# A layer with linear memory: twelve score tiles of a head group in four blocks of three, TensorE's order fixed, masks first

## Chip, cores and metric

The kernel runs on one core of one Trainium2 chip. The metric is device time in microseconds of one execution, as the median of several runs. A core has five engines with queues of their own: TensorE (PE: matmuls; PEld: its weight loads), VectorE (DVE), ScalarE (ACT), GpSimd (POOL) and SyncE (SP), which here issues most DMAs. TensorE writes only to PSUM; VectorE and ScalarE read PSUM and write SBUF.

## The reference

Four layers in the order A, B, A, B on a residual stream x of 2048 tokens by 640. An A layer is attention within four segments of 512 tokens, 32 heads of 20, mixed with a linear memory that is carried from segment to segment:

```python
for s in range(N):                       # 4 segments of L = 512
    logits = jnp.einsum('bhqd,bhkd->bhqk', qs, ks) * scale + mask
    p = _softmax(logits, axis=-1)
    a_dot = jnp.einsum('bhqk,bhkd->bhqd', p, vs)
    pq = phi(qs)                         # phi(t) = t + 1 where t > 0, else exp(t)
    num = jnp.einsum('bhld,bhde->bhle', pq, M)
    den = jnp.einsum('bhld,bhd->bhl', pq, z)[..., None] + 1e-06
    o = g * (num / den) + (1.0 - g) * a_dot
    pk = phi(ks)
    M = M + jnp.einsum('bhld,bhle->bhde', pk, vs)
    z = z + jnp.einsum('bhld->bhd', pk)
...
x = x + _A_ref(_layernorm(x, axis=-1), A_wq, A_wk, A_wv, A_wo, A_beta)
x = x + _B_ref(_layernorm(x, axis=-1), B_mem0, B_Wq, B_Wk, B_Wv, B_Wo, B_seg_len)
```

The mask is causal within the segment. B layers, which the change doesn't touch, are a recurrence over 64 short segments.

## The kernel before

`layer_A` takes the four segments one after the other. In each, the 32 heads are worked in eight groups of four, so that a layer is a loop over 32 groups `g` (`n` is the segment, `G` the group in it), plus two rounds to finish. The loop is a software pipeline (lines 456 to 505): iteration `g` projects q and k of group g+1, computes score tiles of group g, the probabilities of groups g-2 and g-1, and the product with v of group g-2.

Heads lie 32 rows apart, so a group fills 128 rows, and a pair of heads uses two strips of 32 rows of TensorE's array at a time (`tile_position`). A group has two pairs, and a pair p has these tiles, each of two PSUM banks, from a pool of three (`psx`, tag x):

- three S tiles (`s_round`, line 355; matmuls line 372): scores with the queries along the partitions. They serve only for the row maxima, which VectorE takes with reductions (line 375). The causal mask is put in first, by a matmul of the identity with a table of large negative numbers (line 366), and the scores are added to it. Tile 0 holds the last 128 queries against 512 keys, tile 1 two parts (384 and 128 keys), tile 2 one of 256.
- three T tiles (`t_round`, line 394; matmuls line 407): scores with the keys along the partitions, from a copy of q to which the negated maximum has been added (`q_with_max`, line 382). ScalarE takes the exponential into SBUF (line 410), and GpSimd zeroes what is above the diagonal (line 412).

A group so has six S tiles and six T tiles. S of pair p and T of pair p-3 come together; the two pairs lie on different rows of the array. An iteration has six rounds (two halves with `r` = 0, 1, 2), each with one S and one T tile: masks, S matmuls, T matmuls, and then some of the other products:

- `proj_q` (QP, line 276; ScalarE copies to qT and, from segment 1 on, takes EQ, from which VectorE makes phiq), `proj_k` (KP, line 295; ScalarE copies to kT), `proj_v` (VP, line 306; ScalarE copies to one of three `vaug`)
- `q_with_max` (Q2, lines 386 and 388; ScalarE copies to q2)
- `phi_k` (KN, line 318: transposes of k; ScalarE EK, GpSimd clamps it, VectorE phik; all but the last segment)
- `state` (line 327): the read from the memory (NUM, line 333, from segment 1 on; ScalarE copies to nsb, VectorE and GpSimd divide), and the memory's update (UP, line 348, all but the last segment; VectorE masks it, GpSimd adds it)
- `pv` (PV, line 424, 40 matmuls; ScalarE copies to osb), `norm` (VectorE and GpSimd)
- for the segment before, in groups 2 to 5: `out_stage_a` (otps, line 248, transposes; ScalarE copies to oT) and `out_stage_b` (YP, line 259, two halves of 320 columns; VectorE adds x, line 261; two stores on SP's queue)
- for the segment after, in groups 0, 1 and 6: `seg_load` (a load on SP's queue and a layer norm on VectorE and GpSimd, lines 80 to 87) and `seg_tr` (tps, line 236, transposes; ScalarE copies them to xnT)

All these products share a second PSUM pool of two places (`pg`, tag pg, one bank each): a new one must wait until the tile that held its place has been read.

No order is written out for layer A: `A_ORDERED` is False, so a planner arranges each engine's instructions when the program is built, by their order in the source and by its own idea of when each is ready. On the chip each engine then runs its list in that order. In layer B all engines follow the source (`_OrdNC`).

Of the kernel before, what the change touches and what calls it, by code (L numbers as in the profile page):

```python
# [28 lines left out]
D = 640  # L29
# [131 lines left out]
def layer_A(nc, tc, C, W, x_src, x_dst, src_is_bf16, nseg=4, out_bf16=False, xb_dst=None, load_w=None, side_loads=None):  # L161
    SC = 1.0 / math.sqrt(20.0)
    nc_raw = nc
    if A_ORDERED:
        nc = _OrdNC(tc, nc_raw, engines=ORDER_ENGINES)
    NGR = 8 * nseg
    KOFF = (0, 640, 1024, 512)
    assert not out_bf16
    with ExitStack() as ctx:
# [48 lines left out]
        SEG = {}  # L218

        def seg_load(n_, tt):  # L220
            d = SEG.setdefault(n_, {"xn": [None] * 4, "oT": [None] * 4, "xr": [None] * 4})
            r0 = n_ * 512 + tt * 128
            xt = pxt.tile([128, 2 * D] if src_is_bf16 else [128, D], BF16 if src_is_bf16 else F32, name="a_xt")
            nc.sync.dma_start(xt[:, 0:D], x_src[r0:r0 + 128, :])
            xn = pxn.tile([128, D], BF16, name="a_xn")
            layernorm_tile(nc, sml, C, xt[:, 0:D], xn[:], "a_ln")
            d["xn"][tt] = xn
# [20 lines left out]
                nc.tensor.transpose(tps[:, c, :], d["Onat"][:, tt, 128 * c:128 * c + 128], C.identb[:])  # L248
            nc.scalar.copy(oT[:], tps[:])

        def out_stage_b(n_, tt):
            d = SEG[n_]
            oT, xr = d["oT"][tt], d["xr"][tt]
            r0 = n_ * 512 + tt * 128
            xnew = w1l.tile([128, D], F32, name="a_xnew") if src_is_bf16 else xr
            for half in range(2):
                YP = pg.tile([128, 320], F32, name="a_YP", tag="pg")
                for c in range(NCH):
                    nc.tensor.matmul(YP[:], lhsT=oT[:, c, :], rhs=W.wo[:, c, 320 * half:320 * half + 320],
                                     start=(c == 0), stop=(c == NCH - 1))  # L260
                nc.vector.tensor_tensor(out=xnew[:, 320 * half:320 * half + 320], in0=YP[:], in1=xr[:, 320 * half:320 * half + 320], op=ALU.add)
            nc.sync.dma_start(x_dst[r0:r0 + 128, :], xnew[:])
# [61 lines left out]
            nc.vector.scalar_tensor_tensor(out=pk[:, :, :, 0:20], in0=KNv, scalar=0.0, in1=EK[:], op0=ALU.max, op1=ALU.add)  # L324
            GS[g]["pk"] = pk

        def state(g):
            n, G = divmod(g, 8)
            s_ = GS[g]
            if n >= 1:  # L330
                NUM = pg.tile([128, 4, 4, 32], F32, name="a_NUM", tag="pg")
                for tt in range(4):
                    nc.tensor.matmul(NUM[:, tt, :, :].rearrange("p j s -> p (j s)"), lhsT=s_["phiq"][:, 128 * tt:128 * tt + 128],
                                     rhs=MZb[:, G, :], start=True, stop=True)
                nsb = w1.tile([128, 4, 4, 21], F32, name="a_nsb")
                nc.scalar.copy(nsb[:], NUM[:, :, :, 0:21])
# [6 lines left out]
                s_["am"] = am  # L343
            if n <= nseg - 2:
                UP = pg.tile([128, 128], F32, name="a_UP", tag="pg")
                pk, va = s_["pk"], s_["va"]
                for tt in range(4):
                    nc.tensor.matmul(UP[:], lhsT=pk[:, tt, :, :].rearrange("p j s -> p (j s)"),
                                     rhs=va[:, tt, :, :].rearrange("p j s -> p (j s)"), start=(tt == 0), stop=(tt == 3))
# [5 lines left out]
        def s_round(p, r):  # L355
            g, pr = divmod(p, 2)
            s_ = GS[g]
            if pr == 0 and r == 0:
                s_["nm"] = sm.tile([128, 4, 4], F32, name="a_nm", tag="nm")
            qT, kT, nm = s_["qT"], s_["kT"], s_["nm"]  # L360
            X = psx.tile([128, 2, 512], F32, name="a_S", tag="x")
            m0, m1, parts = ((384, 512, ((3, 0, 512),)),
                             (256, 512, ((2, 0, 384), (0, 384, 128))),
                             (128, 256, ((1, 0, 256),)))[r]
            for e in range(2):
                nc.tensor.matmul(X[:, e, m0:m1], lhsT=C.identb[:], rhs=C.negu[:, 0:(m1 - m0) // 128, :].rearrange("p a k -> p (a k)"),
                                 start=True, stop=False, skip_group_check=True)
            for qc, o, w_ in parts:
                for e in range(2):
                    j = 2 * pr + e  # L370
                    rows = slice(32 * j, 32 * j + 32)
                    nc.tensor.matmul(X[:, e, o:o + w_], lhsT=qT[rows, 128 * qc:128 * qc + 128], rhs=kT[rows, 0:w_],
                                     start=False, stop=True, tile_position=(32 * j, 0), skip_group_check=True)
            for qc, o, w_ in parts:
                nc.vector.tensor_reduce(out=nm[:, qc, 2 * pr:2 * pr + 2], in_=X[:, :, o:o + w_], axis=AX.X, op=ALU.max, negate=True)  # L375

        def negmax_rows(g):
# [13 lines left out]
            nc.scalar.copy(q2[:], Q2[:])  # L391
            s_["q2"] = q2

        def t_round(p, r):
# [5 lines left out]
            Y = psx.tile([128, 2, 512], F32, name="a_T", tag="x")  # L400
            parts = (((0, 0, 512),), ((3, 0, 128), (1, 128, 384)), ((2, 0, 256),))[r]
            width, diag = ((512, 1), (512, 2), (256, 1))[r]
            for n_, (kc, o, w_) in enumerate(parts):
                for e in range(2):
                    j = 2 * pr + e
                    rows = slice(32 * j, 32 * j + 32)
                    nc.tensor.matmul(Y[:, e, o:o + w_], lhsT=kT[rows, 128 * kc:128 * kc + 128], rhs=q2[rows, 128 * kc:512],  # L407
                                     start=True, stop=True, tile_position=(32 * j, 0), skip_group_check=True)
            b = 512 * r
            nc.scalar.activation(out=PT[:, :, b:b + width], in_=Y[:, :, 0:width], func=ACT.Exp, scale=SC)  # L410
            dv = PT[:, :, b:b + 128 * diag].rearrange("p e (a q) -> p e a q", q=128)
# [36 lines left out]
        for tt in range(4):  # L448
            seg_load(0, tt)
            if tt == 1:  # L450
                load_w()
            seg_tr(0, tt)
        proj_q(0)
        proj_k(0)

        for g in range(NGR + 2):
            n, G = divmod(g, 8)
            for half in range(2):
                p = 2 * g + half
                for r in range(3):  # L460
                    if g < NGR:
                        s_round(p, r)
                    if 0 <= p - 3 < 2 * NGR:
                        t_round(p - 3, r)
                    k = (half, r)
                    if k == (0, 0) and g + 1 < NGR:
                        proj_q(g + 1)
                    if k == (0, 1):
                        if 0 <= g - 1 < NGR:
                            q_with_max(g - 1)  # L470
                        if n >= 1 and 2 <= G <= 5 and n <= nseg:
                            out_stage_a(n - 1, G - 2)
                        if n + 1 < nseg and G in (0, 1, 6):
                            seg_load(n + 1, min(G, 2))
                            seg_tr(n + 1, min(G, 2))
                    if k == (0, 2) and g + 1 < NGR:
                        proj_k(g + 1)
                    if k == (1, 0) and g < NGR:
                        proj_v(g)
                    if k == (1, 1):  # L480
                        if 0 <= g - 2 < NGR:
                            pv(g - 2)
                        if g < NGR:
                            phi_k(g)
                    if k == (1, 2):
                        if 0 <= g - 2 < NGR:
                            norm(g - 2)
                        if g < NGR:
                            state(g)
                        if n >= 1 and 2 <= G <= 5 and n <= nseg:  # L490
                            out_stage_b(n - 1, G - 2)
                        if n + 1 < nseg and G == 6:
                            seg_load(n + 1, 3)
                            seg_tr(n + 1, 3)
            if g < NGR:
                negmax_rows(g)
# [670 lines left out]
```

## Time and profile before

| | us |
|---|---|
| runs | 2830.86, 2835.52, 2836.12 |
| median | 2835.52 |
| the profiled execution, its time | 2836.99 |
| the profiled execution, its span from first to last instruction | 2835.3 |
| first and last S matmul of the first A layer | 31.6 and 397.7 us into the span |
| first and last S matmul of the second A layer | 1451.3 and 1797.2 us into the span |

A row of the timeline or of a group reads: start and length in us (or line, engine, operation), the tile written and the tiles read, their shapes, how many instructions. `[0.19 <-DVE a_phik L324]` means that the engine had been idle for 0.19 us before, and that the named instruction ended the wait. TensorE's matmuls are pipelined, and the end of each record is modelled, so that starts are compared with starts. The chain of waits is the chain of work that ended last, followed back from the last instruction. A row of stretches has, after the stretch and its length, the busy time and the number of instructions of TensorE, its weight loads, VectorE, ScalarE and GpSimd, then TensorE's granted clock, the busy share of the DMA engines, and GB/s.

### The profile page before, as it was taken

How to read it: one execution, taken by the hardware profiler on the slowest of the kernel's cores; microseconds unless marked ns; L12 is line 12 of the kernel's file. 1: busy time of each engine (PE TensorE's matmuls, PEld its weight loads, DVE VectorE, ACT ScalarE, POOL GpSimd, SP SyncE). 2: the span in 40 equal slices, each digit the busy share in tenths (PEclk: the TensorE clock that was granted, in tenths of full speed). 3: DMA queues.
4: the chain of work that ended last, by engine and by line, in shares of the span. 5: the costliest groups of instructions: out<-in, count | busy, mean ns of one | idle time of the engine just before them, and what ended most of it. 6: DMA issues, size and time to landing. Idle time of an engine off the chain costs nothing.

```text
span 2835.3 us, 147285 instructions
## 1 busy us (share of the span) xinstructions
PE 2667.9 (94%) x65736; PEld 1703.8 (60%) x65736; DVE 1676.5 (59%) x4554; ACT 1567.3 (55%) x3516; POOL 702.8 (25%) x1634
## 2 busy tenths in 40 slices
PE   5899998999999999999979999889999999999998
PEld 2455555666666666666635555556666666666665
DVE  5778864555555555555568878545555555555554
ACT  3777773555555555544448777545555555555443
POOL 3456651111111111111135666411111111111110
PEclk9999999999999999999989999899999999999999
DMA  6110135212221222121130111531211111211110
GB/s 215 53 43 23 39 127 134 44 40 47 44 44 42 43 46 45 41 41 31 31 114 20 57 48 34 174 94 41 43 39 41 41 41 42 43 40 38 39 26 20
DMA packets 322956, 156.54 MB, mean 55 GB/s; under 512 B 245776, under 2 KB 311056, under 8 KB 319248
## 3 DMA queue, kind: packets, MB, share of 16 engines
q1 hardware_dynamic: 320880, 136.63, 19.1%
q8 instruction: 514, 8.42, 1.3%
q10 hardware_dynamic: 1440, 10.49, 1.0%
q14 instruction: 122, 1.00, 0.1%
HBM read 95.65 MB, written 51.38 MB: 52 GB/s over the span
## 4 chain that ended last, share of the span: by engine, by line
PE 54%; DVE 4%; ACT 3%; DMA 2%; issue 1%; POOL 1%; SPq 0%; ACTq 0%; DVEq 0%; POOLq 0%
PE b_OPS L105 7%; PE b_tail L105 4%; PE b_Ka L105 4%; PE b_Qa L105 4%; PE b_Kb L105 4%; PE b_Qb L105 4%; PE b_Va L105 3%; PE b_Vb L105 3%; PE b_SP L105 3%; PE b_OTP L105 2%; PE b_PTP L105 2%; PE b_vtail L105 2%; PE b_OPSd L105 2%; DVE a_nm L375 2%; PE a_QP L276 1%
## 5 line engine op out<-in xcount | busy, mean ns | idle before, releaser
L105 PEld LDWEIGHTS <-b_HX 128*32 128x32 bf16 x15360 | 435.9, 97 | 338.7 <-issue 16.5
L375 DVE TENSOR_REDUCE a_nm<-a_S 128x2 f32<-128x1024 f32 (+3 forms) x512 | 403.7, 811 | 95.1 <-PE a_T L407 71.3
L105 POOL TENSOR_TENSOR b_Pm<-b_E,b_rs 128x96 bf16<-128x96 bf16 x128 | 63.5, 496 | 1446.1 <-ACT b_Vth L105 1082.8
L410 ACT ACTIVATE a_PT<-a_T 128x1024 bf16<-128x1024 f32 (+1 forms) x384 | 340.7, 891 | 51.7 <-PE a_T L407 46.8
L105 PE MATMUL b_OPS<-b_wo,b_OTsb 128*32 128x320 bf16 x8192 | 309.9, 301 | 10.3 <-issue 7.3
L105 PEld LDWEIGHTS <-b_OTsb 128*32 128x32 bf16 x8192 | 201.5, 97 | 97.7 <-DVE b_OTsb L105 25.9
L412 POOL TENSOR_SCALAR_AFFINE_SELECT a_PT<-a_PT 128x256 bf16<-128x256 bf16 (+1 forms) x384 | 198.6, 520 | 235.2 <-ACT a_PT L410 234.0
L105 DVE CAST b_HX<-b_MT 128x8 bf16<-128x8 f32 x372 | 63.7, 172 | 278.5 <-PE b_MT L105 273.4
L105 ACT CAST b_msb<-b_OPS 128x64 bf16<-128x64 f32 x378 | 69.3, 256 | 238.0 <-PE b_OPS L105 238.0
L105 ACT CAST b_kq<-b_Kb 128x512 bf16<-128x512 f32 x128 | 75.0, 586 | 202.4 <-PE b_Kb L105 202.4
L105 DVE COPY b_KT<-b_TPak 128x128 bf16<-128x128 bf16 x128 | 28.8, 225 | 227.2 <-PE b_TPak L105 227.2
L105 PE MATMUL b_Va<-b_wv,b_HX 128*32 128x512 bf16 x2520 | 160.7, 380 | 0.0
L105 PE MATMUL b_Vb<-b_wv,b_HX 128*32 128x512 bf16 x2520 | 160.0, 379 | 0.0
L407 PE MATMUL a_T<-a_q,a_kT 32*128 32x512 bf16 (+3 forms) x1024 | 139.6, 307 | 21.4 <-DVE a_nm L375 14.9
L105 PE MATMUL b_Ka<-b_wk,b_HX 128*32 128x512 bf16 x2520 | 159.0, 379 | 0.0
L105 PE MATMUL b_Kb<-b_wk,b_HX 128*32 128x512 bf16 x2520 | 158.9, 379 | 0.0
L105 PE MATMUL b_Qa<-b_wq,b_HX 128*32 128x512 bf16 x2520 | 158.9, 379 | 0.0
L105 PE MATMUL b_Qb<-b_wq,b_HX 128*32 128x512 bf16 x2520 | 158.9, 379 | 0.0
L105 PEld LDWEIGHTS <-b_kq 128*128 128x128 bf16 x2080 | 116.9, 98 | 69.0 <-ACT b_kq L105 54.8
L105 DVE TENSOR_SCALAR b_kq<-b_Qa 128x512 bf16<-128x512 f32 x128 | 88.5, 692 | 116.7 <-PE b_Qa L105 114.0
L105 DVE CAST b_OTsb<-b_OTP 128x160 bf16<-128x160 f32 (+1 forms) x384 | 122.5, 373 | 40.5 <-PE b_OTP L105 40.3
L105 PE MATMUL b_vtail<-b_wv,b_TX 128*32 128x256 bf16 x2880 | 138.9, 271 | 8.0 <-issue 4.8
(196 smaller groups left out, 5745.1 us busy)
## 6 DMA issues: line engine op xcount, KB each, us to landing
b_QKd<-b_tu SPq DMA_DIRECT2D x128, 128.0 KB
b_tl<-b_QKd SPq DMA_DIRECT2D x128, 128.0 KB
b_wv<-in_B_Wv_dram SPq DMA_DIRECT2D x10, 1024.0 KB
b_wo<-in_B_Wo_dram SPq DMA_DIRECT2D x16, 640.0 KB
b_VTd<-b_vt SPq DMA_DIRECT2D x256, 32.0 KB
b_Vth<-b_VTd SPq DMA_DIRECT2D x512, 16.0 KB
b_XO<-xres SPq DMA_DIRECT2D x256, 30.0 KB
b_wk<-in_B_Wk_dram ACTq DMA_DIRECT2D x5, 1024.0 KB
```

What stands on the lines that cost most here:

```text
L105: r = f(*a, **k)
L276: nc.tensor.matmul(QP[:], lhsT=wqG[:, c, :], rhs=xnT[:, c, :], start=(c == 0), stop=(c == NCH - 1))
L375: nc.vector.tensor_reduce(out=nm[:, qc, 2 * pr:2 * pr + 2], in_=X[:, :, o:o + w_], axis=AX.X, op=ALU.max, negate=True)
L407: nc.tensor.matmul(Y[:, e, o:o + w_], lhsT=kT[rows, 128 * kc:128 * kc + 128], rhs=q2[rows, 128 * kc:512], start=True, stop=True, tile_posi ...
L410: nc.scalar.activation(out=PT[:, :, b:b + width], in_=Y[:, :, 0:width], func=ACT.Exp, scale=SC)
L412: nc.gpsimd.affine_select(out=dv, in_=dv, pattern=[[0, 2], [0, diag], [1, 128]], compare_op=ALU.is_ge, fill=0.0, base=0, channel_multiplie ...
```

## The change

Within `layer_A` only; no product, copy, reduction or DMA is added or left out.

1. TensorE's instructions follow the source (`_OrdNC` for `tensor`). The other engines are still arranged by the planner.
2. Each half has two blocks of three tiles in place of three rounds of two: S0, T0, S2 and then T1, S1, T2. In a block the masks of its S tiles come first, then the matmuls of the three tiles, then one "filler" of other products. An iteration has four blocks and four fillers.
3. `state` is split: the read (`state_num`) stays in group g, the update (`state_up`) is done an iteration later.
4. The other products move: slot 0 has NUM, UP of the group before and QP; slot 1 Q2, KP and otps; slot 2 KN, VP and the first half of YP; slot 3 PV and the second half of YP. `out_stage_b` can do its halves apart.
5. `seg_load` is split into the load and `seg_norm`, the layer norm; for the next segment, load, norm and transposes have slots of their own (`seg_step`).

```diff
-    if A_ORDERED:
-        nc = _OrdNC(tc, nc_raw, engines=ORDER_ENGINES)
+    nc = _OrdNC(tc, nc_raw, engines=("tensor",))
...
+        def seg_step(n, G, slot):
+            if n + 1 >= nseg:
+                return
+            for tt, at in enumerate((((0, 0), (0, 2), (0, 3)), ((0, 3), (1, 2), (1, 3)), ((5, 3), (6, 0), (6, 1)), ((6, 0), (6, 2), (6, 3)))):
+                for f, w_ in zip((seg_load, seg_norm, seg_tr), at):
+                    if w_ == (G, slot):
+                        f(n + 1, tt)
+
+        def filler(g, slot):
+            n, G = divmod(g, 8)
+            out = n >= 1 and 2 <= G <= 5 and n <= nseg
+            if slot == 0:
+                if g < NGR:
+                    state_num(g)
+                if 0 <= g - 1 < NGR:
+                    state_up(g - 1)
+                if g + 1 < NGR:
+                    proj_q(g + 1)
+            elif slot == 1:
+                if 0 <= g - 1 < NGR:
+                    q_with_max(g - 1)
+                if g + 1 < NGR:
+                    proj_k(g + 1)
+                if out:
+                    out_stage_a(n - 1, G - 2)
+            elif slot == 2:
+                if g < NGR:
+                    phi_k(g)
+                    proj_v(g)
+                if out:
+                    out_stage_b(n - 1, G - 2, (0,))
+            else:
+                if 0 <= g - 2 < NGR:
+                    pv(g - 2)
+                    norm(g - 2)
+                if out:
+                    out_stage_b(n - 1, G - 2, (1,))
+            seg_step(n, G, slot)
+
         for g in range(NGR + 2):
             n, G = divmod(g, 8)
             for half in range(2):
-                p = 2 * g + half
-                for r in range(3):
-                    if g < NGR:
-                        s_round(p, r)
-                    if 0 <= p - 3 < 2 * NGR:
-                        t_round(p - 3, r)
...
+                p, tp = 2 * g + half, 2 * g + half - 3
+                for ph in range(2):
+                    items = ((("S", 0), ("T", 0), ("S", 2)), (("T", 1), ("S", 1), ("T", 2)))[ph]
+                    todo = []
+                    for kind, r in items:
+                        if kind == "S" and g < NGR:
+                            todo.append((kind, p, r, s_mask(p, r)))
+                        elif kind == "T" and 0 <= tp < 2 * NGR:
+                            todo.append((kind, tp, r, t_tile()))
+                    for kind, p_, r, X in todo:
+                        (s_mm if kind == "S" else t_round)(p_, r, X)
+                        (s_max if kind == "S" else t_exp)(p_, r, X)
+                    if g < NGR and half == 1 and ph == 1:
+                        negmax_rows(g)
+                    filler(g, 2 * half + ph)
```

More of the change, by code (lines that the diff above doesn't have):

```diff
@@ L249, in out_stage_a, with out_stage_b @@
             nc.scalar.copy(oT[:], tps[:])
-        def out_stage_b(n_, tt):
+        def out_stage_b(n_, tt, halves=(0, 1)):
             d = SEG[n_]
@@ L254, in out_stage_b @@
             r0 = n_ * 512 + tt * 128
-            xnew = w1l.tile([128, D], F32, name="a_xnew") if src_is_bf16 else xr
-            for half in range(2):
+            if 0 in halves:
+                d["xnew"] = w1l.tile([128, D], F32, name="a_xnew") if src_is_bf16 else xr
+            xnew = d["xnew"]
+            for half in halves:
                 YP = pg.tile([128, 320], F32, name="a_YP", tag="pg")
@@ L261, in out_stage_b @@
                 nc.vector.tensor_tensor(out=xnew[:, 320 * half:320 * half + 320], in0=YP[:], in1=xr[:, 320 * half:320 * half + 320], op=ALU.add)
+            if 1 not in halves:
+                return
             nc.sync.dma_start(x_dst[r0:r0 + 128, :], xnew[:])
@@ L343, in state, with state_up @@
                 s_["am"] = am
+        def state_up(g):
+            n, G = divmod(g, 8)
+            s_ = GS[g]
             if n <= nseg - 2:
@@ L367, in s_round, with s_mm @@
                                  start=True, stop=False, skip_group_check=True)
-            for qc, o, w_ in parts:
+            return X
+        def s_mm(p, r, X):
+            g, pr = divmod(p, 2)
+            s_ = GS[g]
+            qT, kT = s_["qT"], s_["kT"]
+            for qc, o, w_ in S_SPAN[r][2]:
                 for e in range(2):
@@ L392, in q_with_max, with t_tile, t_round @@
             s_["q2"] = q2
-        def t_round(p, r):
+        def t_tile():
+            return psx.tile([128, 2, 512], F32, name="a_T", tag="x")
+        def t_round(p, r, Y):
             g, pr = divmod(p, 2)
```

66 lines of the change are left out of this document (23 added, 43 removed).

## The prediction

> **What bounds the kernel now.** I read busy time by stretches first, then the chain of waits in order of time, then the timeline of one group, TensorE alone. The change is confined to the two A layers, so the question is what limits a group there. A stretch of the second one (us; busy us of TensorE, its weight loads, VectorE, ScalarE, GpSimd; clock):
>
> ```profile
> 1560.00:1600.00 40.00, 38.20 (x497) 22.29 (x494) 30.27 (x65) 30.18 (x51) 24.16 (x51) 1.00 0.18 63
> ```
>
> TensorE is busy 38.2 of 40 us at full clock; VectorE and ScalarE have a quarter in reserve. The chain of waits gives a group's period, from the same product in neighbouring groups:
>
> ```profile
> 1500.03 1.08 PE a_QP L276 x5
> ...
> 1509.81 1.08 PE a_QP L276 x5
> ...
> 1521.89 1.25 PE a_QP L276 x5
> ...
> 1638.82 1.24 PE a_KP L295 x5
> ...
> 1649.34 1.24 PE a_KP L295 x5
> ...
> 1749.23 1.20 PE a_QP L276 x5
> ...
> 1760.10 1.20 PE a_QP L276 x5
> ```
>
> First segment: 9.78 us, and 12.08 where a group also takes in rows of the next segment. Middle segments without an output tile: 10.52. Last segment with one: 10.87. A middle group with an output tile is below, UP to UP: 12.22.
>
> ```profile
> 1575.03 0.40 PE L348 MATMUL a_UP<-a_vaug,a_phik 128*128 128x128 bf16 x4 [0.19 <-DVE a_phik L324]
> ...
> 1575.94 0.38 PE L366 MATMUL a_S<-c_negu,c_identb 128*128 128x256 bf16 x2
> ...
> 1576.64 0.84 PE L259 MATMUL a_YP<-a_wo,a_oT 128*128 128x320 bf16 x5
> 1577.35 1.24 PE L276 MATMUL a_QP<-a_xnT,a_wq_pad 128*128 128x512 bf16 x5
> 1578.52 0.23 PE L372 MATMUL a_S<-a_kT,a_qT 32*128 32x128 bf16 x2
> ...
> 1578.85 0.39 PE L386 MATMUL a_Q<-a_qT,c_identb 128*128 128x512 bf16 x1
> ...
> 1579.30 0.28 PE L366 MATMUL a_S<-c_negu,c_identb 128*128 128x128 bf16 x2
> 1579.76 0.44 PE L248 MATMUL a_otps<-c_identb,a_Onat 128*128 128x128 bf16 x5 [0.18 <-ACT a_EQ L282]
> 1580.13 0.28 PE L372 MATMUL a_S<-a_kT,a_qT 32*128 32x256 bf16 x2
> ...
> 1581.20 1.25 PE L295 MATMUL a_KP<-a_xnT,a_wk_pad 128*128 128x512 bf16 x5
> 1582.39 0.39 PE L407 MATMUL a_T<-a_q,a_kT 32*128 32x512 bf16 x2
> 1582.71 0.89 PE L306 MATMUL a_VP<-a_wv,a_xnT 128*128 128x80 bf16 x20
> 1583.43 0.38 PE L366 MATMUL a_S<-c_negu,c_identb 128*128 128x256 bf16 x2
> 1583.75 0.34 PE L372 MATMUL a_S<-a_kT,a_qT 32*128 32x384 bf16 x2
> ...
> 1584.09 1.17 PE L424 MATMUL a_PV<-a_vaug,a_PT 128*128 128x32 bf16 x40
> 1585.10 0.38 PE L318 MATMUL a_KN<-c_identb,a_kT 128*128 128x128 bf16 x4
> 1585.32 0.27 PE L366 MATMUL a_S<-c_negu,c_identb 128*128 128x128 bf16 x2
> ...
> 1585.83 0.38 PE L333 MATMUL a_NUM<-a_MZb,a_phiq 128*128 128x128 bf16 x4
> 1586.06 0.28 PE L366 MATMUL a_S<-c_negu,c_identb 128*128 128x128 bf16 x2
> ...
> 1587.25 0.40 PE L348 MATMUL a_UP<-a_vaug,a_phik 128*128 128x128 bf16 x4 [0.19 <-DVE a_phik L324]
> ```
>
> Read start to start, almost nothing is idle: two waits, 0.18 and 0.19. From 1575.94 to 1582.71 lie 6.77; less YP 0.71, QP 1.17, Q2 0.45, otps 0.37, KP 1.19 and the wait 0.18, 2.70 are left for masks and tiles. From 1583.43 to 1587.25 lie 3.82; less PV 1.01, KN 0.22, NUM 0.23 and the wait 0.19, 2.17. Together 4.87 of the 12.22 go to twelve tiles. A tile's matmuls use 32 rows of the array, masks and the other products 128, and the seam shows: QP takes 1.17 when a tile follows it, while its record (1.24) less the 0.16 by which a record outlasts the next start (YP: 0.84 against 0.68 from 1575.26) is 1.08: so 0.1 a seam. Where S and T stand together they run side by side: S of 384, T of 128 and 384 and S of 128 columns take 0.34 (1583.75 to 1584.09).
>
> By the Trainium skill, "TensorEngine Tiling (Array Packing)", section "Key Properties", a change of tiling mode drains the array. Eight seams fewer a group are 0.8 us by the row's 0.1; if a drain laid bare the whole 0.16, they would be 1.3, and the trace has the smaller.
>
> **What the change removes, adds and moves.** *Six rounds to four blocks.* Per block: masks of 512 columns in all 0.22 and a seam 0.1; two wide tiles on different rows side by side 0.22, the third 0.11, the seam back 0.1. That is 0.75, four times 3.0 against 4.87: 1.87 less. If tiles don't overlap, a block is 0.2 dearer; if seams are free, 0.2 cheaper; I take 0.75, nearest to the 0.34 piece. QP, KP, otps and the first YP no longer touch a tile and lose 0.1 each. TensorE's work is then 9.6 us with output (UP and NUM 0.23 each, QP and KP 1.08 each, Q2 0.45, otps 0.27, KN 0.22, VP 0.72, YP twice 0.68, PV 1.01, blocks 3.0) and 8.0 without.
>
> *What is late next.* All products share two places in PSUM, all tiles three. With TensorE's order fixed, a product waits for the evacuation of an earlier one, and that stands behind a block's exponentials on ScalarE (count, busy us, mean ns):
>
> ```profile
> L410 ACT ACTIVATE a_PT<-a_T 128x1024 bf16<-128x1024 f32 x124 | 127.0, 1025 | 21.7 <-PE a_T L407 19.4
> L410 ACT ACTIVATE a_PT<-a_T 128x512 bf16<-128x512 f32 x61 | 37.7, 618 | 3.0 <-PE a_T L407 2.6
> ...
> L391 ACT CAST a_q<-a_Q 128x512 bf16<-128x512 f32 x31 | 18.5, 597 | 0.1
> L282 ACT ACTIVATE a_EQ<-a_QP 128x512 bf16<-128x512 f32 x24 | 14.5, 602 | 0.0
> L309 ACT CAST a_vaug<-a_VP 128x320 bf16<-128x320 f32 x32 | 13.7, 427 | 0.6 <-PE a_VP L306 0.6
> ...
> L336 ACT COPY a_nsb<-a_NUM 128x336 f32<-128x336 f32 x24 | 10.8, 452 | 0.0
> L321 ACT ACTIVATE a_EK<-a_KN 128x320 f32<-128x320 bf16 x24 | 10.6, 442 | 0.4 <-PE a_KN L318 0.4
> ```
>
> I walk a middle group with output from its first mask at 0; neighbours on ScalarE overlap by 0.1, and 0.05 lies from an end to the waiter. Block 0 ends at 0.75; NUM and UP at 1.2. T0's exponential runs 0.8 to 1.8, NUM's copy to 2.15, so QP starts at 2.2: **1.0 lost**. QP to 3.27, block 1 to 4.02, Q2 to 4.46. KP needs QP's place, which EQ reads to 4.6: 0.2 lost. KP to 5.71. otps needs Q2's place, whose copy stands behind EQ and the exponentials of T1 and T2 and ends at 6.53: **0.9 lost**. otps and block 2 to 7.58, KN and VP to 8.57. The first YP needs VP's place, whose copy stands behind otps's, T0's exponential and EK until 9.4: **0.9 lost**. YP to 10.11, block 3 to 10.86, PV 11.87, YP 12.55. So 12.55 against 12.22: 0.33 slower here, though TensorE works 2.2 us less.
>
> The same walk elsewhere. Middle without output: 8.0 and waits of 1.0 (QP), 0.2 (KP), 0.5 (T0 of block 2 on q2), 0.4 (first mask on T2's exponential): 10.16 against 10.52. Last segment: without UP, QP finds a free place; 9.15 and 1.05 of waits are 10.2 against 10.87, and I give its groups without output the same 0.65. First segment: no NUM, 8.6 against 9.78.
>
> *Sum per layer.* First segment, the five groups after the start: 5 x 1.15 = 5.8. Middle: 8 x 0.36 = 2.9 and 8 x -0.33 = -2.6. Last: 8 x 0.65 = 5.2. That is 11.3, and 22.6 for two layers. The layer norm of the next segment now stands a slot or more ahead of its transposes; today such a group costs 2.3 more (12.08 against 9.78). Three per layer: bounds 0 and 2.3 each, I take 1.2, since the norm's VectorE time stays: 7 in all. The loads are as many DMAs as before on SP's queue, one to three slots (some 2.5 us each) ahead of their norm. One of them lands in 3.0:
>
> ```profile
> 1547.28 3.03 DMA a_xt<-xres
> ```
>
> One, at the end of group 5, is written right behind the output tile's two stores; if it queues behind them and they wait for the result, its transposes come about 2 late, six times 2 = 12 at most; I take none, since it needs nothing of theirs. Output tiles split into halves are the same matmuls in two slots, at no price.
>
> *The clock* may take some back (columns as in the first fence):
>
> ```profile
> 1720.00:1725.00 5.00, 2.94 (x74) 2.12 (x71) 2.79 (x8) 2.66 (x4) 1.21 (x3) 0.93 0.74 132
> 1725.00:1730.00 5.00, 4.47 (x29) 1.75 (x25) 4.74 (x13) 2.56 (x5) 2.20 (x5) 0.50 0.29 4
> ```
>
> Five us with TensorE busy 2.94 are followed by five at half clock. The waits of 0.9 to 1.0 lie apart; I charge 3 us. 22.6 + 7 - 3 = 27. The profiled execution took 2837.0 (span 2835.3), 1.5 over the median 2835.5 of the three runs: **2809**.
>
> **Rivals.** *Slower: KN's place.* If the first YP, or PV in groups without output, gets KN's place and not VP's, it waits for the longest evacuation: EK, a clamp on GpSimd, then phik on VectorE behind two maxima.
>
> ```profile
> L324 DVE SCALAR_TENSOR_TENSOR a_phik<-a_KN,a_EK 128x320 bf16<-128x320 bf16 x24 | 11.8, 490 | 3.1 <-POOL a_EK L322 1.8
> ...
> L322 POOL TENSOR_SCALAR a_EK<-a_EK 128x320 f32<-128x320 f32 x24 | 10.9, 454 | 11.6 <-ACT a_EK L321 11.6
> ```
>
> In the walk EK ends at 9.05, the clamp at 9.55, phik at 10.1 against 9.4 for VP: 0.7 more; without output PV waits behind one maximum more, 1.1 more, in the first segment 1.0. Per layer 8 x 0.7 + 8 x 1.1 + 5 x 1.0 = 19.4, twice 39: 2848. It decides from 27 us on, two thirds of such groups. For it: UP waits for phik today (0.19). Against: VP's copy is sooner, and nothing ties YP to KN.
>
> *Slower or even: the clock.* One half-clock stretch of 3.4 us costs up to 1.7 of TensorE's time; one in each of the 16 middle groups with output is 27 us: 2836. For it: 2 idle in 5 were enough above. Against: the walk's worst 3.4 us hold 1.3 of waits. The Trainium skill, "TensorE: Matmul & The Clock Gate", "Why this matters for your kernels", warns of gaps over about 3 us; by it none of these waits would count, but the row shows less to be enough.
>
> *Much faster: the waits are hidden*, because copies run ahead of exponentials. Then work sets the time: 9.6 with output (VectorE's 30.27 of 40 is 9.25 a group, so no lower), about 8.7 without, 8.0 and 8.9 in first and last segments: 8 x 2.6 + 8 x 1.8 + 5 x 1.8 + 8 x 1.8 = 58 a layer, 2720. Against: the exponential's tile is ready before NUM, Q2 and VP are.
>
> *Nothing comes of it*: S and T already overlap in half the rounds, and the waits eat the rest: 2830 to 2841.
>
> **How the numbers follow.** Forecast 0.50, its own range 2790 to 2828; KN's place 0.18; clock 0.12; hidden waits 0.10; nothing 0.10. The range 2758 to 2858 leaves out most of the hidden waits and the far end of the slower cases. This kernel's measurement tells 0.2% (5.7 us) from no change: faster 0.62 (forecast, hidden waits, a little of the clock), same 0.12, slower 0.26.
>
> **What would show it.** Right: blocks of about 0.75 with S and T starting together; QP idle about 1 us before it in middle groups, released by the copy of NUM or UP; first YP released by VP's copy; periods near 8.6, 10.2, 12.5 and 10.2. Wrong: middle groups under 11 (hidden waits), a product released by phik (KN's place), clock under 1 in the middle of a layer, or masks waiting long for exponentials.

## The result, and the profile after

The changed kernel takes 2819.95 us (median of 6 runs, 2811.09 to 2822.41) against 2833.35 (6 runs, 2826.18 to 2838.94) for the kernel before on the same chip: a ratio of 0.9955, 95% interval 0.9939 to 0.997. That is 13 us where 27 were forecast. The profiled execution after took 2819.05 us, its span 2817.2, against 2835.3: 18.1 less.

The stretch of middle groups in the second A layer, whose row before read 38.20 of 40 us for TensorE, and two five-us stretches earlier in the layer (us; busy us of TensorE, its weight loads, VectorE, ScalarE, GpSimd; clock):

```profile
1600.00:1640.00 40.00, 35.00 (x521) 21.52 (x522) 34.59 (x65) 32.96 (x56) 25.84 (x53) 1.00 0.01 2
1500.00:1505.00 5.00, 3.42 (x44) 2.11 (x43) 4.58 (x8) 3.44 (x6) 2.43 (x5) 1.00 0.02 6
1505.00:1510.00 5.00, 4.27 (x70) 2.38 (x70) 4.13 (x10) 3.63 (x7) 3.54 (x9) 0.66 0.00 0
```

TensorE now has 5 us in 40 with nothing to do, and VectorE is as busy as it. The last two rows show a stretch with 1.58 us idle and, in the next stretch, a clock of 0.66; what idled there comes below. One middle group with an output tile, TensorE's timeline (start, us, instruction, in brackets the idle time before it and what ended it):

```profile
1638.82 0.40 PE L105 MATMUL a_NUM<-a_MZb,a_phiq 128*128 128x128 bf16 x4
1639.17 0.38 PE L105 MATMUL a_UP<-a_vaug,a_phik 128*128 128x128 bf16 x4
1640.26 1.24 PE L105 MATMUL a_QP<-a_xnT,a_wq_pad 128*128 128x512 bf16 x4 [0.71 <-ACT a_nsb L344]
1641.34 0.38 PE L105 MATMUL a_S<-c_negu,c_identb 128*128 128x256 bf16 x2
1641.65 0.23 PE L105 MATMUL a_T<-a_q,a_kT 32*128 32x128 bf16 x2
1641.66 0.34 PE L105 MATMUL a_S<-a_kT,a_qT 32*128 32x384 bf16 x2
...
1642.08 0.39 PE L105 MATMUL a_Q<-a_qT,c_identb 128*128 128x512 bf16 x1
...
1642.67 1.24 PE L105 MATMUL a_KP<-a_xnT,a_wk_pad 128*128 128x512 bf16 x5
1644.56 0.44 PE L105 MATMUL a_otps<-c_identb,a_Onat 128*128 128x128 bf16 x5 [0.65 <-ACT a_q L413]
...
1645.82 0.88 PE L105 MATMUL a_VP<-a_wv,a_xnT 128*128 128x80 bf16 x20
1647.41 0.84 PE L105 MATMUL a_YP<-a_wo,a_oT 128*128 128x320 bf16 x5 [0.71 <-ACT a_vaug L317]
...
1652.71 0.38 PE L105 MATMUL a_QP<-a_xnT,a_wq_pad 128*128 128x512 bf16 x1 [0.71 <-ACT a_nsb L344]
```

QP to QP is 12.45. A block is 0.74 (1641.34 to 1642.08), S and T start together, and the three waits are those of the prediction's walk through a group, with the releasers it named. A wait in brackets begins where the record before it ends, 0.16 behind the point where the next instruction could have started, so from start to start the three cost 0.87, 0.81 and 0.87. Two shorter waits hide inside the records. KP starts 0.05 after the exponential EQ has read QP's place (1642.02 to 1642.62), and UP 0.05 after VectorE has read the second YP (1638.64 to 1639.12). In the first segment, where nothing takes EQ, Q2's start to KP's is 0.45 (1480.19 to 1480.64) and not 0.59; without an output tile NUM's start to UP's is 0.23 (1605.47 to 1605.70) and not 0.35. The waits of TensorE in most of that layer, by what was waited for (us in total, times, longest):

```profile
PE a_QP L105 <- ACT a_nsb L344: 13.0, 17, 0.9
PE a_T L105 <- DVE a_nm L397: 9.8, 9, 2.5
PE a_otps L105 <- ACT a_q L413: 7.7, 12, 0.6
PE a_YP L105 <- ACT a_vaug L317: 5.7, 8, 0.8
```

The second row is in no term of the forecast: T waiting for a maximum.

Where most of the 18.1 us of the span came from can be read off one instruction of each group, the copy of QP on ScalarE. Its first and last of each layer, before and then after:

```profile
28.11 0.59 ACT L278 CAST a_qT<-a_QP 128x512 bf16<-128x512 f32 x1 [2.38 <-PE a_QP L276]
383.51 0.59 ACT L278 CAST a_qT<-a_QP 128x512 bf16<-128x512 f32 x1
1447.70 0.59 ACT L278 CAST a_qT<-a_QP 128x512 bf16<-128x512 f32 x1 [2.44 <-PE a_QP L276]
1783.06 0.59 ACT L278 CAST a_qT<-a_QP 128x512 bf16<-128x512 f32 x1
```

```profile
27.81 0.59 ACT L286 CAST a_qT<-a_QP 128x512 bf16<-128x512 f32 x1 [2.38 <-PE a_QP L105]
369.69 0.59 ACT L286 CAST a_qT<-a_QP 128x512 bf16<-128x512 f32 x1 [0.23 <-PE a_QP L105]
1431.93 0.59 ACT L286 CAST a_qT<-a_QP 128x512 bf16<-128x512 f32 x1 [2.44 <-PE a_QP L105]
1765.05 0.59 ACT L286 CAST a_qT<-a_QP 128x512 bf16<-128x512 f32 x1 [0.24 <-PE a_QP L105]
```

The first layer gained 13.5, the second 2.2; of the other 2.4 us, about 2 lie between the two layers, where nothing was changed. By segment (eight periods each, seven in the last), from the same instruction:

| us | segment 0 | 1 | 2 | 3 |
|---|---|---|---|---|
| first A layer, before | 92.4 | 95.5 | 91.9 | 75.5 |
| first A layer, after | 78.8 | 93.9 | 93.5 | 75.6 |
| second A layer, before | 75.5 | 92.6 | 91.8 | 75.4 |
| second A layer, after | 66.9 | 99.0 | 92.1 | 75.1 |

Segment 0 gave it all: 13.6 in the first layer, where the forecast had 5.8, and 8.5 in the second. The middle segments came out even in the first layer and lost 6.7 in the second; the last segments came out about even.

### The profile page after: what moved, and what is told of

It reads as the page before. It is cut to its first block, busy times and chain, and to the rows that moved or that the text cites. A ratio compares the mean times of both kernels' runs of the same rounds, so it can differ in the third digit from the quotient of the medians.

```text
span 2817.2 us, 147274 instructions
## 1 busy us (share of the span) xinstructions
PE 2597.5 (92%) x65670; PEld 1686.8 (60%) x65736; DVE 1703.3 (60%) x4554; ACT 1559.2 (55%) x3516; POOL 701.6 (25%) x1634
## 3 DMA queue, kind: packets, MB, share of 16 engines
q10 hardware_dynamic: 1440, 10.49, 1.0%
## 4 chain that ended last, share of the span: by engine, by line
PE 52%; DVE 4%; ACT 4%; DMA 2%; issue 2%; POOL 1%; SPq 0%; DVEq 0%; ACTq 0%; POOLq 0%
PE b_OPS L105 7%; PE b_tail L105 4%; PE b_Ka L105 4%; PE b_Kb L105 4%; PE b_Qa L105 4%; PE b_Qb L105 4%; PE b_Va L105 3%; PE b_Vb L105 3%; PE b_SP L105 3%; PE b_OTP L105 2%; PE b_OPSd L105 2%; PE b_PTP L105 2%; PE b_vtail L105 2%; ACT a_PT L439 2%; DVE a_nm L397 2%
## 5 line engine op out<-in xcount | busy, mean ns | idle before, releaser
L105 PEld LDWEIGHTS <-b_HX 128*32 128x32 bf16 x15360 | 428.5, 97 | 341.2 <-issue 12.0
L397 DVE TENSOR_REDUCE a_nm<-a_S 128x2 f32<-128x1024 f32 (+3 forms) x512 | 395.8, 815 | 34.8 <-PE a_S L105 15.8
L439 ACT ACTIVATE a_PT<-a_T 128x1024 bf16<-128x1024 f32 (+1 forms) x384 | 325.2, 887 | 100.0 <-PE a_T L105 48.4
L441 POOL TENSOR_SCALAR_AFFINE_SELECT a_PT<-a_PT 128x256 bf16<-128x256 bf16 (+1 forms) x384 | 189.4, 509 | 221.7 <-ACT a_PT L439 220.8
L105 PE MATMUL a_T<-a_q,a_kT 32*128 32x512 bf16 (+3 forms) x1024 | 122.2, 311 | 24.9 <-DVE a_nm L397 19.8
```

Of the source, the lines that this page charges most:

```text
L105: r = f(*a, **k)
L441: nc.gpsimd.affine_select(out=dv, in_=dv, pattern=[[0, 2], [0, diag], [1, 128]], compare_op=ALU.is_ge, fill=0.0, base=0, channel_multiplie ...
```

## The experiments

Each ratio is to the kernel before on the same chip (its medians there were 2817 to 2823 us), with its 95% interval; "the period" is again from one copy of QP to the next. Three questions: which part of the change did what, what each of the waits costs, and what held back the groups in which the forecast failed.

**Order alone.** The kernel before with `nc = _OrdNC(tc, nc_raw, engines=("tensor",))` in place of the switch that is off.

> The kernel before with one line of the change: TensorE's order fixed as the program writes it, still six rounds of two tiles. Theory (the order is what creates the waits on evacuations, the blocks are what pays for them): slower than before by 0.5 to 4%, 2848 to 2945 us, TensorE idle before products whose place another product holds. Rival (the fixed order by itself is harmless or gives the gain of the first layer's start): 2815 to 2835 us.

Measured: 1.0106 (1.0088 to 1.0124), slower, as the theory had it; middle periods 12.42 and 11.06 (before 12.22 and 10.52). TensorE's largest wait:

```profile
PE a_UP L105 <- DVE a_phik L323: 27.5, 23, 2.0
```

UP stood right behind KN in the written order and waited 1.2 us on average for phik. In the changed kernel UP comes a group later, and no product of the loop waits for phik, save one transposition at the start (2.5 us). That the split alone pays for the fixed order is likely, but no run has it by itself.

**Blocks with the planner's order.** The kernel after with one line less; all else of the change stays.

```diff
-    nc = _OrdNC(tc, nc_raw, engines=("tensor",))
```

> The kernel after with TensorE's order left to the planner; blocks, split output tile, spread norms stay. Theory (the waits of 0.65 to 0.9 before QP, otps and the first YP belong to the fixed order): the planner fills them, groups with an output tile fall from 12.45 to about 11, 2785 to 2805 us. Rival (the planner pulls the blocks apart again, so that S and T stand alone and seams return): 2820 to 2850 us, groups at 12 and more.

Measured: 0.9992 (0.9979 to 1.0004): no gain at all, the rival. The waits for copies shrink (YP's for VP's copy from 5.7 us to 1.4 in the second layer), but middle groups take 12.86 and 11.01. The planner put the wide products into the blocks, and masks then wait for maxima, 14.6 us in 21 places of that layer:

```profile
1648.09 0.38 PE L377 MATMUL a_S<-c_negu,c_identb 128*128 128x256 bf16 x2 [0.75 <-DVE a_nm L396]
1648.40 0.39 PE L430 MATMUL a_T<-a_q,a_kT 32*128 32x128 bf16 x3
1648.72 1.25 PE L283 MATMUL a_QP<-a_xnT,a_wq_pad 128*128 128x512 bf16 x5
1649.90 0.33 PE L430 MATMUL a_T<-a_q,a_kT 32*128 32x384 bf16 x1
```

QP sits between two halves of one block. Blocks and order belong together: without the order the rest of the change gives nothing, and the order alone costs 1%.

**One place for NUM and UP.**

```diff
-                NUM = pg.tile([128, 4, 4, 32], F32, name="a_NUM", tag="pg")
+                NU = pg.tile([128, 512], F32, name="a_NU", tag="pg")
...
-                UP = pg.tile([128, 128], F32, name="a_UP", tag="pg")
+                UP = NU[:, 336:464]
```

In the lines not shown, NUM writes 84 columns in place of 128 per matmul, so that both fit into one bank.

> The kernel after, but NUM (84 columns of each 128 written, the other 44 are zeros that nothing reads) and UP share one place in PSUM, so QP finds the other place free. Theory (QP's wait for the copy of NUM, 13.0 us in 17 places of the second layer, is a loss of its own): about 0.8 less in each middle group, 32 groups in two layers, 26 us: 2790 to 2800 us, middle groups at 9.6 and 11.6. Rival (the wait only moves: Q2, otps, the masks or YP take it up, since ScalarE's queue sets them all): middle groups at 10.2 to 10.4 and 12.2 to 12.4, 2812 to 2820 us.

Measured: 0.9978 (0.9967 to 0.999), middle periods 12.68 and 10.6: longer than in the kernel after. QP waits for nothing now, but UP does, in front of it:

```profile
1653.81 0.38 PE L105 MATMUL a_NU<-a_vaug,a_phik 128*128 128x128 bf16 x4 [1.12 <-ACT a_nsb L345]
1654.03 1.24 PE L105 MATMUL a_QP<-a_xnT,a_wq_pad 128*128 128x512 bf16 x5
```

UP writes columns 336 to 463 and NUM's copy reads 0 to 335, and still UP's matmuls wait for the copy: here the dependence went by the whole tile, which is one bank. The wait moved one product ahead. This says nothing against QP's wait being a loss of its own; the next one does the test without a shared tile.

**QP between NUM and UP.**

```diff
                     state_num(g)
+                if g + 1 < NGR:
+                    proj_q(g + 1)
                 if 0 <= g - 1 < NGR:
                     state_up(g - 1)
-                if g + 1 < NGR:
-                    proj_q(g + 1)
```

> The kernel after with QP written between NUM and UP, so that UP and not QP takes the place that NUM's copy frees. Theory (QP's wait of 0.9 is only that the two short products take both places ahead of it): QP covers the copy, UP waits 0.1 to 0.2, middle groups 9.7 and 11.8 in place of 10.4 and 12.45, 32 of them make 20 us: ratio to before 0.987 to 0.990, 2797 to 2805 us on a chip where before takes 2833. Rival (as with the shared place, the wait turns up again in a later product because ScalarE's queue sets the pace): ratio 0.994 to 0.998.

Measured: 0.9887 (0.9865 to 0.991); middle periods 11.86 and 9.2 to 10.4. The theory holds: 1.08 us of QP covers the copy of NUM, and UP runs behind it without a wait. What comes next is Q2, which stands behind VectorE's evacuation of UP (the row a_upm), and that has maxima and the divisions of NUM's copy ahead of it:

```profile
1638.87 1.24 PE L105 MATMUL a_QP<-a_xnT,a_wq_pad 128*128 128x512 bf16 x4
1639.96 0.38 PE L105 MATMUL a_UP<-a_vaug,a_phik 128*128 128x128 bf16 x4
1641.78 0.38 PE L105 MATMUL a_Q<-a_qT,c_identb 128*128 128x512 bf16 x1 [0.79 <-DVE a_upm L363]
1643.29 0.44 PE L105 MATMUL a_otps<-c_identb,a_Onat 128*128 128x128 bf16 x5
```

In turn otps, later now, no longer waits for q2, but the T tile of the next block does: it starts 0.42 behind its S tile (1643.89, 1644.31), and the block takes 1.06 and not 0.74. So two waits, 0.87 and 0.81, became one of 0.86 and one of 0.32, and KP's hidden 0.14 is gone. Hence 0.6 and not 1.7 in a group with output.

**KN last in its slot.**

```diff
-                    phi_k(g)
                     proj_v(g)
                 if out:
                     out_stage_b(n - 1, G - 2, (0,))
+                if g < NGR:
+                    phi_k(g)
```

> The kernel after with the third slot's products in the order VP, YP, KN (was KN, VP, YP). Theory (YP waits 0.7 to 0.77 for VP's copy because VP took the place that YP needs; in the other order YP has KN's old place and KN waits for the copy): middle groups with output 11.8 in place of 12.45, 16 of them, 10 us: ratio to before 0.991 to 0.993. Rival (KN, EK, the clamp and phik then come 0.9 later, and PV or UP waits for that): ratio 0.995 to 1.0, groups at 12.4 to 12.8.

Measured: 0.9946 (0.9926 to 0.9965). YP's wait for VP's copy is gone, and the period with output is 11.82, as the theory said; but the total shows 2.5 of the 10 us, too little to tell from nothing by these intervals, since groups without output rose from 10.4 to 10.7 and those of segment 0 from 8.64 to 8.91. Each side saw half.

**Layer B's norm behind layer A's last maximum.** An ordering edge on VectorE, no data moved:

```diff
-            layernorm_tile(nc, sml, C, xt[:], xt[:], "b_ln")
+            first = layernorm_tile(nc, sml, C, xt[:], xt[:], "b_ln")
+            if g == 0 and W.after_max is not None:
+                tc.add_manual_dep(first.ins, W.after_max.name, ...)
```

> The kernel after, with VectorE made to start layer B's first norm behind the last maximum of layer A. Theory (the last segment's groups 24 and 25 lost their gain to that norm, in whose shadow T waits 2.5 for a maximum): the period of 12.2 to 12.4 falls to about 10.0 and the one before it to 9.8, 3 us a layer, 6 in all, if layer B's start still finds the norm done in layer A's tail: ratio to before 0.993 to 0.994. Rival (that stall is VectorE's own load of maxima, or what is saved comes back at layer B's start): period stays above 11.5, or ratio 0.995 to 0.998.

Measured: 0.9921 (0.9902 to 0.9941). In the kernel after, VectorE and TensorE at the group that took 12.22:

```profile
1713.45 0.91 DVE L105 TENSOR_SCALAR b_xt<-b_xt,b_ln_mv,b_ln_rstd 128x640 bf16<-128x640 bf16 x1 [0.45 <-POOL b_ln_rstd L105]
1714.29 1.13 DVE L294 SCALAR_TENSOR_TENSOR a_phiq<-a_EQ,a_rq 128x512 bf16<-128x512 bf16 x1
1715.34 3.00 DVE L397 TENSOR_REDUCE a_nm<-a_S 128x2 f32<-128x768 f32 x4
```

```profile
1716.67 0.42 PE L105 MATMUL a_T<-a_q,a_kT 32*128 32x512 bf16 x2 [2.50 <-DVE a_nm L397]
```

VectorE takes its queue in order. It waits for layer B's norm (on GpSimd) while block 1's maxima stand behind it, the places of the tiles stay taken, and T waits 2.5. With the norm behind, the two periods 10.49 and 12.22 became:

```profile
1691.45 0.58 ACT L287 CAST a_qT<-a_QP 128x512 bf16<-128x512 f32 x1 [1.33 <-PE a_QP L106]
1700.36 0.58 ACT L287 CAST a_qT<-a_QP 128x512 bf16<-128x512 f32 x1
1709.83 0.58 ACT L287 CAST a_qT<-a_QP 128x512 bf16<-128x512 f32 x1
```

8.91 and 9.47, 4.3 us a layer. The ratio fell by 0.0034, 9.6 us, though by the intervals this may be some 7 us more or less. Nothing shows that it came back at layer B's start: from the last copy of QP in the first A layer to the first in the second lie 1057.6 us, and 1062.2 in the kernel after.

The kernel before pays for the same norm. Its group there takes 13.55 (second of the segment), with VectorE and then TensorE:

```profile
1721.55 0.89 DVE L105 BATCH_NORM_STATS2 b_ln_st<-b_xt 128x6 f32<-128x320 bf16 x2 [1.51 <-DMA b_xt<-xres_bf]
1723.61 0.39 PE L407 MATMUL a_T<-a_q,a_kT 32*128 32x128 bf16 x4 [2.06 <-DVE a_nm L375]
```

What the same edit would give the kernel before was not run.

**Layer B's weights on SyncE's queue**, in the kernel before and in the kernel after:

```diff
-            nc.scalar.dma_start(t[:, G, :], ...)
+            nc.sync.dma_start(t[:, G, :], ...)
```

> The kernel before, with layer B's weights in the first layer issued on SyncE's queue and not on ScalarE's. Theory (the 13.6 us that the first segment of the first layer lost in the change came from ScalarE's queue: three of its copies of QP stood 3.5 to 3.8 us behind an issue of these weights that waits for the load before it): 10 to 14 us faster than before, 2819 to 2823 us, groups 3 to 5 of that segment at about 10 in place of 13.5. Rival (those groups waited for TensorE's order or for the loads themselves): within 3 us of before.

> The kernel after, with layer B's weights issued on SyncE's queue, as in the run on the kernel before, which then won 16 to 18 us in the first segment. Theory (most of what the change won lay there, and the same loads still cost the kernel after two groups of 13.9 and 13.6): 9 to 12 us faster than after, ratio to before 0.991 to 0.992, so that the change is worth only 0.2 to 0.3% against the kernel before with the same edit (0.9942). Rival (the change's gain is its own, and the loads cost both kernels the same): 16 us faster than after, ratio 0.989 to 0.990.

Measured: before 0.9942 (0.9923 to 0.996), after 0.9919 (0.99 to 0.9938). Of before, a copy of QP in segment 0 of the first layer, one of three such, a group apart:

```profile
74.71 0.59 ACT L278 CAST a_qT<-a_QP 128x512 bf16<-128x512 f32 x1 [3.59 <-DMA b_wq<-in_B_Wq_dram]
```

Such groups took 13.5. The profile names a weight load as releaser; but the copies were not held up by it. Ahead of each, TensorE waits for maxima, then runs QP at half clock (0.50 in 73 to 75), and the copy starts as soon as QP is done, here at 74.68:

```profile
71.27 0.38 PE L366 MATMUL a_S<-c_negu,c_identb 128*128 128x256 bf16 x2 [1.31 <-DVE a_nm L375]
72.34 2.34 PE L276 MATMUL a_QP<-a_xnT,a_wq_pad 128*128 128x512 bf16 x5
```

From 28 to 110 us, masks wait for maxima 11.7 us in 12 places, and with the loads moved 1.2 us in two. In the kernel after only two groups, 13.91 and 13.57, still pay. There VectorE stands 3.04 us (at 46.53) and 1.76 (at 56.98) for a load of x for the layer norm; a mask waits 3.66 and 2.05 for the maxima behind it, and at 49.03 an exponential stands 4.63 behind a weight issue that itself waits for GpSimd, where the same norm comes first. So the runs show what the place of the weight issues is worth, but not through which wait: with the issues on another queue the planner also laid out the lists of VectorE and, in the kernel before, of TensorE anew.

With the loads moved, the segment takes 72.7 us before and 65.6 after (92.4 and 78.8 with them). From first to last copy of QP, the two kernels then differ by 6.4 us in the first layer and nothing in the second, 8.6 in the whole span; by time 0.9942 against 0.9919, intervals that overlap. So about half of the measured gain, by one profile of each kernel, can be had without the change, by moving the loads; and that one line in the kernel before (0.9942) is worth as much as the whole change (0.9955).

**Norm left out.**

```diff
-            layernorm_tile(nc, sml, C, xt[:, 0:D], xn[:], "a_ln")
+            if n_ == 0:
+                layernorm_tile(nc, sml, C, xt[:, 0:D], xn[:], "a_ln")
+            else:
+                nc.gpsimd.tensor_copy(xn[:], xt[:, 0:D])
```

> The kernel after with the layer norm of segments 1 to 3 left out in both A layers: a plain cast on GpSimd stands in its place, so the output is another. Theory (the groups that take in rows lose their gain because T waits behind the norm's work on VectorE, 1.0 to 1.6 at a time, and a half-clock stretch follows): T's waits for a maximum there go, the period of the group before the middle segment falls from 10.65 to about 8.8, the first ones of that segment from 12.7 and 12.0 to 10.5 to 11, the last from 13.3 to 10.5, some 8 us a layer: ratio to before 0.989 to 0.991. Rival (loads, transposes and their copies are what those groups pay for): less than 3 us a layer, ratio 0.993 to 0.996.

Measured: 0.9888 (0.9874 to 0.9901). In the second layer the periods 10.65, 12.72, 12.02 and 13.31 became 9.41, 10.55, 10.5 and 11.1, its sum 10 us less; T's waits for a maximum in those groups went from 5.5 us to 0.3. In the kernel after, VectorE and then TensorE:

```profile
1500.73 0.49 DVE L80 BATCH_NORM_STATS2 a_ln_st<-a_xt 128x6 f32<-128x320 f32 x1 [0.38 <-DMA a_xt<-xres]
1501.14 1.07 DVE L294 SCALAR_TENSOR_TENSOR a_phiq<-a_EQ,a_rq 128x512 bf16<-128x512 bf16 x1
1502.14 1.28 DVE L397 TENSOR_REDUCE a_nm<-a_S 128x2 f32<-128x768 f32 x2
```

```profile
1503.47 0.39 PE L105 MATMUL a_T<-a_q,a_kT 32*128 32x512 bf16 x2 [1.49 <-DVE a_nm L397]
```

The norm stands at the head of VectorE's queue, waiting for its load; the maxima wait behind it, T behind them, and the half-clock row of 1505 to 1510 follows. The run takes both away, the norm's work and its wait for the load, so it does not tell how much is each; in the first layer the start changed as well (68.5 for 78.8). The kernel before was not run without its norm, so what the norm costs there is not known.

**Four edits together, and two additions**: QP between, KN last, layer B's norm late, its weights on SyncE.

> The kernel after with four edits together: QP between NUM and UP, KN last in its slot, layer B's norm behind layer A's last maximum, layer B's weights on SyncE's queue. Theory (they mend four separate losses, so they add up): 0.9955 less 0.0068, 0.001, 0.0034 and 0.0036 is a ratio of 0.981, middle groups with output at 11.2, where Q2's wait for upm and the first YP's for VP's copy no longer stand one behind the other. Rival (with one wait gone the next takes its place, as where NUM and UP shared a place): ratio 0.984 to 0.987, middle groups with output at 11.8.

Measured: 0.9798 (0.9785 to 0.9811), 2757.44 us: the fastest of all, and faster than both kernels. The gains add up, and middle groups with output take 11.23, as expected.

The output tile's transposes at the end of the last slot of the group before:

```diff
-                if out:
-                    out_stage_a(n - 1, G - 2)
...
+                if n >= 1 and 1 <= G <= 4 and n <= nseg:
+                    out_stage_a(n - 1, G - 1)
```

> The same four edits, and the output tile's transposes in the last slot of the group before. Theory (since QP stands between NUM and UP, otps finds Q2's copy done; its old wait is already gone): no gain by itself beyond 0.1%, ratio within 0.001 of the run with four edits. Rival (three products in a slot always cost the third one a wait): middle groups with output 0.3 shorter, 16 of them 5 us, ratio 0.002 lower.

Measured: 0.9884 (0.987 to 0.9897). Later groups take 11.24, no gain, as the theory said, but each first output tile of a segment takes 14 to 16: its transposes now come in the same slot as the last group's PV and wait for the result of that (1.92 and, a segment later, 3.08 for the row on GpSimd that writes a_Onat). Neither side had that.

UP out of the first slot, to the head of the second:

```diff
             if slot == 0:
...
-                if 0 <= g - 1 < NGR:
-                    state_up(g - 1)
...
             elif slot == 1:
+                if 0 <= g - 1 < NGR:
+                    state_up(g - 1)
                 if 0 <= g - 1 < NGR:
                     q_with_max(g - 1)
```

> The four edits, with UP not behind QP but first in the second slot, ahead of Q2. Theory (Q2 waited 0.78 for VectorE to evacuate UP behind block 0's maxima; now the place that Q2 takes is QP's, free when EQ ends, and only KP needs UP's): 0.3 to 0.6 less in each of 32 middle groups, 10 to 19 us under the run with four edits, ratio 0.974 to 0.978. Rival (upm is as late as before behind block 1's maxima, and KP waits in place of Q2): ratio as with four edits or above.

Measured: 0.9944 (0.9931 to 0.9956), middle 12.08 and 10.78. The rival, and worse: three products now stand in that slot, and KP is the one that waits for a copy behind two exponentials.

```profile
1648.54 1.24 PE L106 MATMUL a_KP<-a_xnT,a_wk_pad 128*128 128x512 bf16 x5 [1.28 <-ACT a_q L415]
```

## Why the prediction was right, and where it was not

*The bound and the blocks: right.* A block of 0.75 was taken, 0.74 is there, with S and T of one block starting 0.01 apart.

*The walk: right, nearly term by term.* Middle with output 12.45 (12.55), without 10.4 (10.16), segment 0 8.64 (8.6), last segment 10.3 to 10.6 (10.2). QP's 1.0, otps's 0.9 and YP's 0.9 are 0.87, 0.81 and 0.87, each with its releaser. KP's 0.2 is 0.14, and a wait that the walk did not have, UP's for the read of YP, is 0.12; less these, 9.64 is left for the work of 9.6. Without output, QP waits 1.05 from start to start (1605.70 to 1606.98, less 0.23), and the blocks in which the walk lets T0 and the first mask wait, 0.5 and 0.4, are longer by 0.4 to 0.6 each (1.18 and 1.32 in place of 0.74, at 1600.08 and 1604.15). As gains are differences of two such sums, the small errors count: groups without output gained about 0.1 and not 0.36, those with output lost 0.23 and not 0.33. The Trainium skill, "Perfetto Trace Analysis", "Optimization Strategy", says that the same gap repeating on an engine that should be saturated can mean too little SBUF or PSUM for the next tile. The trace agrees so far as the gap repeats, 0.71 or 0.89 ahead of QP in group after group; yet here a change of order among the same two places took 0.59 off the period of 12.45.

*Groups without output in the last segment, "I give its groups without output the same 0.65": the step that failed.* 5.2 a layer was forecast for this segment; it came out 0.1 longer in the first layer and 0.4 shorter in the second, though the groups with output do gain 0.3 to 0.6 each. Its first three periods, without output, take 33.3 in the second layer (10.56, 10.49, 12.22) against 32.0 before. The walk held only layer A's work, and VectorE runs layer B's first norm there: with that norm moved two of them take 8.91 and 9.47, and the segment 71.1 where the kernel before takes 75.5. But that kernel's figure holds the same norm's stall, so how much of these 4.4 us is the change's own is not shown.

*Layer norm groups, "I take 1.2": the term failed, in the second layer in sign too.* The walk looked at TensorE and ScalarE; in these groups VectorE's queue decides. The second layer's middle segments lost 6.7 us, and the first layer's came out even, where the terms add up to a gain of 2.7 (0.3, and two such groups); without the norm the second layer's sum is 10 us shorter. What was right is that "the norm's VectorE time stays". A likely reason for the miss, argued and not shown, is that a fixed TensorE order has nothing to put in T's place while VectorE is held up.

*The start of the first layer, taken as none: gained 13.6 in its segment 0*, where 5.8 was forecast for both layers alike. The cause lies with the weight loads of layer B: with them moved, the segment's gain is 7.1 (72.7 to 65.6). Through which wait they cost the kernel before more is open. With the loads moved in both kernels the change is worth 0.2%, by intervals that overlap.

*The clock: not settled.* 3 us were charged; the mean granted clock of the whole execution is 0.981 after and 0.979 before, but in the second A layer alone it is 0.97 (1431 to 1783) against 0.98 (1447 to 1800), and 0.01 of 352 us is 3.5. By the rounding of these two it could be as well twice that or next to nothing.

*The rivals.* KN's place: fell, in the second layer YP is released by VP's copy in all 8 places. The clock in middle groups: fell, 1.00 in 1600 to 1640. Hidden waits: fell, all three are there; the runs with changed orders recover a part. Nothing comes of it: true of the blocks with the planner's order. So the forecast's sign and its middle groups rest on the right mechanism. That the total came out on the forecast's side at all is in good part luck: about half of the gain came from a place that the forecast had left out, and it made up for the last segment and the norm groups, where the forecast gains did not come.

## What to carry to other kernels

With an order fixed by hand and few places for results, put a long product between two short ones, so that the evacuation of the first is covered before the third needs its place; here that alone was worth 0.7% (0.9955 to 0.9887). Walk every queue that feeds the stage, the next stage's early work and the issues of loads included: here a norm that waited at the head of VectorE's queue held up the maxima behind it, and T behind them. And when a change wins, ask in which stage: here about half of it could be had without the change. A releaser that the profile names is not yet the cause: look at when the other input was ready, as with the copies of QP behind a QP at half clock.

## What was not expected of the hardware

A stretch of 5 us with TensorE busy 3.42 was followed by a clock of 0.66 in the next 5 (rows of 1500 to 1510), though its longest wait is 1.49. On VectorE the same instruction can take half as long again: phiq's 128x512 took 1.13 at 1714.29 and 0.72 at 1745.58.

```profile
1745.58 0.72 DVE L294 SCALAR_TENSOR_TENSOR a_phiq<-a_EQ,a_rq 128x512 bf16<-128x512 bf16 x1
```

GpSimd is busy at both times, and no run here tells the cause apart.
